# Moving the right-hand pools of a fused attention and two-MoE kernel by 160 and 224 bytes

## The chip, the cores and the metric

The kernel runs on one core of one Trainium2 chip. The metric is the device time of one execution in microseconds; several executions are timed and the median is given. One more execution is profiled, and the trace is of that one.

## The reference

Attention for 4 batches of 8 heads, 576 positions, 64 per head, with a threshold: scores more than tau below their row's largest are cut off before the softmax. Its output, 2304 tokens of 512, goes through two feed-forward layers of width 2048, all in float32.

```python
scores = scale * np.matmul(q, k.transpose(0, 1, 3, 2))
thresh = np.max(scores, axis=-1, keepdims=True) - tau
scores = np.where(scores >= thresh, scores, -1000000000.0)
attn = np.exp(scores - np.max(scores, axis=-1, keepdims=True))
attn = attn / (np.sum(attn, axis=-1, keepdims=True) + 1e-09)
x = np.matmul(attn, v)                       # to [2304, 512]
h = x @ moe_w_in;  x = (h * np.clip(h + 3.0, 0.0, 6.0) / 6.0) @ moe_w_out
h = x @ moe2_w_in; x = (h / (1.0 + np.exp(-1.702 * h))) @ moe2_w_out
```

## The kernel before

Every float32 matrix is split into a high and a low part that TensorE reads in its fast float32 form, and a product is made of three matmuls: high by high, high by low and low by high (`xh`, `xl`, `inhring`, `inlring` and so on). The stages overlap. Up to some 400 us, attention runs pair of heads by pair of heads: scores into PSUM tile `ps` (line 807, and 831 and 847 for the first batch), maximum, exponential and threshold into `e` (lines 863 to 867), transposes (`pk`, `et`, `tr`), the product with the values (lines 1009 and 1025). The first layer's first half of the weights is multiplied in between (lines 1087 and 1112, the helpers `gated` and `out_mm`). From 400 us to 650 us comes the first layer's second half (1087, 1112 and the wide form, 1202). From 650 us on comes the second layer in two passes, in a form with seven products in place of eight on quarter blocks (`hidden2`, line 1321, and the product with the second matrix, line 1457).

The order of the work is worked out while the program is built. A planner (`Plan`) holds every operation with its engine and its dependencies; a packed table of ranks (`RANKS`) and a table of exchanged engines (`SWAPS`) decide the order. Each engine gets its own queue, in which instructions run in the written order and wait on semaphores. All large transfers are issued from SyncE's queue.

On-chip memory is filled from two ends. Pools are opened on the left (`const`, then `LEFT` and `MIDDLE`, later `LAST`) and on the right (`RIGHT` during attention, then `LATE`, then `END` and `xv`). A pool that is closed gives its room to the next one on its side. A constant of 4 bytes takes 32, and a tile's size is otherwise a multiple of 64, nearly always of 256, so a whole side has one remainder. These are the addresses in bytes within a partition, as the program's build places them:

| pool | side | first and last byte's end | remainder of a tile's start modulo 256 |
|---|---|---|---|
| const: id, id2, two, tau, sc, nt, big, half, gate | left | 16,512 to 18,208 | 128 (id, two, tau), others differ |
| ring1: weights, first ring | left | 18,208 to 83,744 | 32 |
| gp, tp: g, t | left | 83,744 to 109,344 | 32 |
| xr, x1: attention's result, its parts | left | 109,344 to 132,384 | 32 |
| gl, ct (after xr and x1 are closed) | left | 109,344 to 134,944 | 32 |
| raw, st, e, et (attention) | right | 154,848 to 229,344 | 224 |
| bt, stg or tr (attention) | right | 138,208 to 154,848 | 224, and 32 past a multiple of 64 |
| ring2: weights, second ring (after attention) | right | 163,808 to 229,344 | 224 |
| yc, stg2, later xs with xab or xv | right | 135,136 to 163,808 | 224 |

The change touches the lists of pools, `change()`, which closes attention's pools and opens those of `LATE`, the line that makes the small constants (545), and the operation `TL` (line 1654). `TL` runs one activation of the kind that the second layer needs, on a single column, behind the last exponential of attention; its result, written to `gate_b`, is read by nobody.

Of the kernel before, what the change touches and what calls it, by code (L numbers as in the profile page):

```python
# [10 lines left out]
F32 = mybir.dt.float32  # L11
# [4 lines left out]
ACTF = mybir.ActivationFunctionType  # L16
# [3 lines left out]
P = 128  # L20


PE, ACT, DVE, POOL, SP, DMA = range(6)
# [377 lines left out]
def tile_top_attention_moe_moe2(  # L401
# [13 lines left out]
    nc = tc.nc  # L415
# [13 lines left out]
    LEFT = ("ring1", "gp", "tp")  # L429
    MIDDLE = ("xr", "x1")  # L430
    RIGHT = ("raw", "st", "e", "et", "bt", "stg")
    LATE = ("ring2", "yc", "stg2", "py")
    LAST = ("gl", "ct")
    END = ("xs", "xab")
    attention, middle, staging, staging2, blocks = (ExitStack() for _ in range(5))
    pools = {n: ctx.enter_context(tc.tile_pool(name=n, bufs=1)) for n in ("const",) + LEFT}
    pools.update((n, middle.enter_context(tc.tile_pool(name=n, bufs=1))) for n in MIDDLE)
    pools["pm"] = ctx.enter_context(tc.tile_pool(name="pm", bufs=1, space=PS))
    for n in RIGHT:
        pools[n] = (staging if n == "stg" else attention).enter_context(tc.tile_pool(name=n, bufs=1, side="right"))  # L440
# [6 lines left out]
    def change():  # L447
        attention.close()
        for n in LATE:
            pools[n] = (staging2 if n == "stg2" else ctx).enter_context(tc.tile_pool(name=n, bufs=1, space=PS) if n == "py" else tc.tile_pool(name=n, bufs=1, side="right"))  # L450

    def change2():
        middle.close()
        for n in LAST:
            pools[n] = ctx.enter_context(tc.tile_pool(name=n, bufs=1))
# [10 lines left out]
    pl = Plan()  # L466
    changed = []

    def add(eng, cost, time, name, fn, rd=(), wr=(), touch=(), alt=None):
        op = pl.add(eng, cost, time, fn, rd, wr, name, touch)  # L470
        op.alt = alt
        for c, names in changed:
            if any(b.pool in names for b in op.bufs):
                op.deps.add(c)
        return op

    def move(time, name, nbytes, fn, rd=(), wr=(), eng=SP):

        op = add(eng, 590, time, name, fn, rd, wr)
        add(DMA, nbytes / 360 * PACE.get(name, 1.0), time, name, lambda: None, rd, wr).deps.add(op)  # L480

    def buf(tag, ring, pool, shape, dt=F32):
        b = Buf(pl, tag, ring, None, pool)
        b.make = lambda: pools[pool].tile(shape, dt, tag=f"{tag}{b.idx % ring}" if ring > 1 else tag, name=tag, bufs=1)
        return b
# [22 lines left out]
    def const(name, shape):  # L508
        b = buf(name, 1, "const", shape)
        b.t  # L510
        return b
# [30 lines left out]


    id_b, id2_b, two_b = const("id", [P, P]), const("id2", [P, 64]), const("two", [P, P])
    tau_b, sc_b, nt_b, big_b, half_b, gate_b = (const(n, [P, 64 if n == "gate" else 1]) for n in ("tau", "sc", "nt", "big", "half", "gate"))
    move(-30000, "tau", 4 * P, lambda: nc.sync.dma_start(out=tau_b.t, in_=tau), [], [tau_b])
    move(-25000, "id", 4 * P * P, lambda: nc.sync.dma_start(out=id_b.t, in_=ident), [], [id_b])
    add(DVE, 69, -30000, "sc", lambda: nc.vector.tensor_scalar(out=sc_b.t, in0=tau_b.t, scalar1=0.0, scalar2=scale, op0=ALU.is_ge, op1=ALU.mult), [tau_b], [sc_b])
# [1008 lines left out]
    t, u = 0, 0  # L1557
    for b in range(B):
        halves_ = []
        for j in range(H // 2):  # L1560
            halves_.append(unit(u, b, j, t))
            if u < FULL:
                halves_[j](0)
                t, u = t + 2700 * 4, u + 1
            else:
                halves_[j]()
                t, u = t + 2700 * 9, u + 1
# [8 lines left out]
        else:  # L1576
            for p in range(2):
                moe_a(b, p, t + 6000)

    changed.append((add(SP, 0, 0, "change", change), LATE))  # L1580
    changed[-1][0].deps |= {o for o in pl.ops if any(x.pool in RIGHT + ("tr", "ps") for x in o.bufs)}
    chunks = [(B - 1, 0), (B - 1, 1)]
# [68 lines left out]
                fetch(w[i], kept[4 + i], t - 30000 + 9000 * i)  # L1651
                w[i] = products(w[i])

    add(ACT, 1500, t, "TL", lambda: nc.scalar.activation(out=gate_b.t[:, :1], in_=half_b.t, func=ACTF.Gelu_apprx_sigmoid), [half_b], [gate_b]).deps |= {o for o in pl.ops if o.name == "X"}

    def tie(ins, first):
        if ins is not None and first is not None:
# [68 lines left out]
```

## Time and profile before

| | |
|---|---|
| median of 3 runs | 1023.88 us |
| lowest and highest run | 1023.46 and 1024.68 us |
| the profiled execution | 1023.98 us |
| its span, first to last instruction | 1022.2 us |
| TensorE busy | 1009.4 us, 99% of the span |
| VectorE, ScalarE, GpSimd busy | 80%, 65%, 54% |

The span is shorter than the execution's own time by what lies before the first and after the last instruction. "Busy" counts from an instruction's start to its end; matmuls are pipelined, so their ends overlap and a busy TensorE can still be slower or faster per matmul. In the chain that ended last, a piece of one line with its count of matmuls gives the time from matmul to matmul.

### The profile page before, as it was taken

Reading aid. Unit: us, or ns where it says so; the run is one execution under the profiler, and the core shown is the slowest. Engines: PE = TensorE matmul, PEld = TensorE weight load, DVE = VectorE, ACT = ScalarE, POOL = GpSimd, SP = SyncE. Lnnn points to the kernel's source line nnn. Section 1 sums busy time; section 2 is a strip of 40 time slices with the busy share of each in tenths; the row PEclk is TensorE's granted clock in tenths of the full one; section 3 lists DMA queues with packets and bytes.
Section 4 is the critical chain, followed back from the end, with each engine's and each line's share of the span. In section 5 each row is a group of like instructions: output and inputs, shape, how many; then the busy total and the mean of one; then the engine's idle time right before and its main releaser. Section 6 shows DMA issues by size and latency. Waiting matters only on the chain.

```text
span 1022.2 us, 21304 instructions
## 1 busy us (share of the span) xinstructions
PE 1009.4 (99%) x7530; PEld 942.7 (92%) x7530; DVE 813.3 (80%) x1728; ACT 668.6 (65%) x1399; POOL 547.0 (54%) x661
## 2 busy tenths in 40 slices
PE   8999999999999999999999999999999999999998
PEld 6787888798979898999999999999999999999998
DVE  7999999999889994678888767757688988665654
ACT  5998887776776765655455443567667767555563
POOL 5677776665756543656434344355544345536432
PEclk9999999999999999999999999999999999999999
DMA  8434476685868665446766665837465896443412
GB/s 234 122 115 144 140 193 179 178 230 176 250 193 220 181 201 159 134 150 206 241 190 213 199 206 181 291 129 244 160 212 193 269 300 209 154 156 106 154 41 83
DMA packets 114059, 187.45 MB, mean 183 GB/s; under 512 B 10913, under 2 KB 64289, under 8 KB 111905
## 3 DMA queue, kind: packets, MB, share of 16 engines
q1 hardware_dynamic: 113808, 185.80, 59.1%
q8 instruction: 59, 0.97, 0.4%
q14 instruction: 48, 0.39, 0.1%
q10 hardware_dynamic: 144, 0.29, 0.1%
HBM read 117.77 MB, written 68.29 MB: 182 GB/s over the span
## 4 chain that ended last, share of the span: by engine, by line
PE 90%; DVE 4%; DMA 3%; ACT 2%; issue 1%; SPq 0%; POOL 0%; DVEq 0%; ACTq 0%
PE pm L1321 17%; PE pm L1087 11%; PE py L1457 10%; PE pm L1112 9%; PE py L1112 8%; PE pm L1202 7%; PE ps L807 6%; PE pm L1457 6%; PE pm L1025 5%; PE pm L933 4%; PE pm L1009 2%; PE ps L831 1%; PE ps L847 1%; PE pm L1029 1%; DMA kept<-inhring 1%
## 5 line engine op out<-in xcount | busy, mean ns | idle before, releaser
L863 DVE TENSOR_REDUCE nm<-ps 128x1 f32<-128x576 f32 x144 | 106.0, 749 | 12.2 <-PE ps L807 7.3
L535 POOL TENSOR_TENSOR g<-t,g 128x256 fp32r<-128x256 f32 (+2 forms) x84 | 73.0, 870 | 79.4 <-ACT g L532 43.5
L866 ACT ACTIVATE e<-ps,nm 128x576 f32<-128x576 f32 x128 | 93.0, 737 | 29.5 <-DVE nm L863 25.6
L1112 PE MATMUL pm<-g,outhring 128*128 128x256 f32 (+1 forms) x512 | 106.8, 300 | 0.0
L867 DVE SCALAR_TENSOR_TENSOR e<-ps,th,e 128x576 f32<-128x576 f32 x128 | 102.4, 809 | 4.9 <-ACT e L866 3.4
L532 ACT ACTIVATE g<-t 128x256 fp32r<-128x256 f32 (+3 forms) x173 | 83.5, 489 | 28.3 <-DVE t L1214 14.9
L1112 PE MATMUL py<-g,outhring 128*128 128x432 f32 (+2 forms) x384 | 97.2, 337 | 1.0 <-DVE yc L535 0.6
L1087 PE MATMUL pm<-xh,inhring 128*128 128x256 f32 (+1 forms) x320 | 97.1, 303 | 0.2
L1087 PE MATMUL pm<-xl,inhring 128*128 128x256 f32 (+1 forms) x320 | 94.4, 295 | 0.0
L1087 PE MATMUL pm<-xh,inlring 128*128 128x256 f32 (+1 forms) x320 | 94.4, 295 | 0.0
L535 POOL TENSOR_TENSOR wmstg<-wmstg,wrstg 128x512 uint32<-128x512 uint32 x40 | 55.4, 1388 | 66.1 <-DVE wmstg L589 28.8
L1112 PEld LDWEIGHTS pm<-g,outhring 128*128 128x128 f32 x512 | 82.0, 189 | 2.9 <-issue 2.5
L807 PE MATMUL ps<-kqv 128*128 128x288 f32 x480 | 81.4, 302 | 1.4 <-DVE e L867 0.5
L1112 PE MATMUL pm<-g,outlring 128*128 128x256 f32 (+1 forms) x256 | 75.8, 296 | 0.1
L807 PEld LDWEIGHTS ps<-kqv 128*128 128x128 f32 x480 | 68.1, 190 | 7.6 <-PE pm L1029 2.0
L1112 PEld LDWEIGHTS py<-g,outhring 128*128 128x128 f32 x384 | 68.2, 188 | 4.1 <-DVE yc L535 0.9
L535 POOL TENSOR_TENSOR kqv<-qk,kqv 128x576 fp32r<-128x576 f32 (+1 forms) x39 | 56.4, 1446 | 19.2 <-PE pm L1029 8.4
L1400 ACT ACTIVATE t<-c 128x512 f32<-128x512 f32 (+1 forms) x80 | 46.2, 582 | 31.0 <-DVE c L535 29.9
L1112 PE MATMUL py<-g,outlring 128*128 128x432 f32 (+2 forms) x192 | 64.6, 336 | 0.0
L1087 PEld LDWEIGHTS pm<-xh,inhring 128*128 128x128 f32 x320 | 60.5, 189 | 2.7 <-PE pm L1667 0.7
L1087 PEld LDWEIGHTS pm<-xl,inhring 128*128 128x128 f32 x320 | 60.5, 189 | 0.0
L1087 PEld LDWEIGHTS pm<-xh,inlring 128*128 128x128 f32 x320 | 60.4, 189 | 0.0
(316 smaller groups left out, 3571.9 us busy)
## 6 DMA issues: line engine op xcount, KB each, us to landing
turned<-tr SPq DMA_DIRECT2D x16, 1024.0 KB, 4.0
et<-turned SPq DMA_DIRECT2D x64, 256.0 KB, 6.2
wrawstg<-in_w1i_dram SPq DMA_DIRECT2D x16, 512.0 KB, 4.1
wrawstg<-in_w1o_dram SPq DMA_DIRECT2D x16, 512.0 KB, 3.8
wrawstg<-in_w2i_dram SPq DMA_DIRECT2D x16, 512.0 KB, 4.0
wrawstg<-in_w2o_dram SPq DMA_DIRECT2D x16, 512.0 KB, 4.1
qk<-in_k_dram SPq DMA_DIRECT2D x24, 288.0 KB, 3.4
qk<-in_q_dram SPq DMA_DIRECT2D x24, 288.0 KB, 3.8
```

What stands on the lines that cost most here:

```text
L532: return lambda: nc.scalar.activation(out=o(), in_=i(), func=ACTF.Copy, **kw)
L535: return lambda: (nc.vector if eng == DVE else nc.gpsimd).tensor_tensor(out=o(), in0=a(), in1=b(), op=op)
L807: nc.tensor.matmul(ps.t[:, i, :SH], q, w[hd].t[:, i * SH:(i + 1) * SH], start=a, stop=z)
L863: add(DVE, 672, K("R", s), "R", lambda: nc.vector.tensor_reduce(out=nm.t[:, c], in_=ps.t[:, :, :SH], op=ALU.max, axis=AX.XY, negate=True), ...
L866: add(ACT, 624, K("X", s), "X", lambda: nc.scalar.activation(out=ev(), in_=ps.t[:, :, :SH], func=ACTF.Exp, bias=nm.t[:, c]), [ps, (nm, s)] ...
L867: add(DVE, 736, K("M", s), "M", lambda: nc.vector.scalar_tensor_tensor(out=ev(), in0=ps.t[:, :, :SH], scalar=th.t[:, c], in1=ev(), op0=ALU ...
L1025: nc.tensor.matmul(pv[p].t[64 * hd:64 * hd + 64, :CH[p][1]], v_(k, hd), et_m(p, turned)[:, hd, k], start=k == 0, stop=False)
L1087: nc.tensor.matmul(ph.t[:, :n], a, v, start=(cc == 0 and i == 0), stop=(cc == KC - 1 and i == 2))
L1112: nc.tensor.matmul(py.t[:, :n], a, v, start=(st and i == 0), stop=(sp and i == 2))
L1202: nc.tensor.matmul(ph.t[:, :n], a, v, start=(cc == 0 and q == 0), stop=(cc == KC - 1 and q == 2))
L1321: nc.tensor.matmul(half(i)(), u.t[:, ws], v.t[:, xv], start=False, stop=True, skip_group_check=True)
L1457: nc.tensor.matmul(to, u.t[:, ws], v.t[:, at:at + n], start=(st and j == 0 and cc == 0 and o is not None), stop=(sp and j == 2), skip_grou ...
```

## The change

Two tiles of padding that nothing uses are put on the right side: `edge`, 40 floats (160 bytes), ahead of all right pools, for the whole program; and `gap`, 16 floats (64 bytes), between the second ring and the pools below it, from `change()` on. `TL`'s result goes to tau's tile, and the tile `gate`, 64 floats, is no longer made. The operations, their engines and their order stay.

```diff
-    LATE = ("ring2", "yc", "stg2", "py")
+    LATE = ("ring2", "gap", "yc", "stg2", "py")
...
+    pools["edge"] = ctx.enter_context(tc.tile_pool(name="edge", bufs=1, side="right"))
+    pools["edge"].tile([P, 40], F32, tag="edge", name="edge", bufs=1)
     pools["pm"] = ctx.enter_context(tc.tile_pool(name="pm", bufs=1, space=PS))
     for n in RIGHT:
...
         for n in LATE:
             pools[n] = (staging2 if n == "stg2" else ctx).enter_context(tc.tile_pool(name=n, bufs=1, space=PS) if n == "py" else tc.tile_pool(name=n, bufs=1, side="right"))
+        pools["gap"].tile([P, 16], F32, tag="gap", name="gap", bufs=1)
...
-    tau_b, sc_b, nt_b, big_b, half_b, gate_b = (const(n, [P, 64 if n == "gate" else 1]) for n in ("tau", "sc", "nt", "big", "half", "gate"))
+    tau_b, sc_b, nt_b, big_b, half_b = (const(n, [P, 1]) for n in ("tau", "sc", "nt", "big", "half"))
...
-    add(ACT, 1500, t, "TL", lambda: nc.scalar.activation(out=gate_b.t[:, :1], in_=half_b.t, func=ACTF.Gelu_apprx_sigmoid), [half_b], [gate_b]).deps |= {o for o in pl.ops if o.name == "X"}
+    add(ACT, 1500, t, "TL", lambda: nc.scalar.activation(out=tau_b.t, in_=half_b.t, func=ACTF.Gelu_apprx_sigmoid), [half_b], [tau_b]).deps |= {o for o in pl.ops if o.name == "X"}
```

## Rows read from the trace of the kernel before

**Rows 1.** The page's head: span, busy time by engine, TensorE's granted clock by slice.
```profile
span 1022.2 us, 21304 instructions
...
PE 1009.4 (99%) x7530; PEld 942.7 (92%) x7530; DVE 813.3 (80%) x1728; ACT 668.6 (65%) x1399; POOL 547.0 (54%) x661
...
PEclk9999999999999999999999999999999999999999
```

**Rows 2.** The page's chain that ended last, shares by engine.
```profile
PE 90%; DVE 4%; DMA 3%; ACT 2%; issue 1%; SPq 0%; POOL 0%; DVEq 0%; ACTq 0%
```

**Rows 3.** Waits of TensorE's matmuls: us in total, times, longest us.
```profile
PE pm L1667 <- DVE two L553: 1.4, 1, 1.4
PE pm L933 <- DVE et L937: 1.1, 1, 1.1
PE ps L831 <- DMA qk<-in_k_dram: 1.1, 1, 1.1
...
PE py L1457 <- DVE gl L535: 0.2, 1, 0.2
```

**Rows 4.** The tile gate: duration in ns, first and last start in us.
```profile
L1654 ACT ACTIVATE gate<-half x1: 204/204/204, 388.7 to 388.7; 128x1 f32<-128x1 f32 x1
```

**Rows 5.** The tile tau, its last reader.
```profile
L550 DVE TENSOR_SCALAR nt<-tau,big x1: 210/210/210, 4.7 to 4.7; 128x1 f32<-128x1 f32 x1
```

**Rows 6.** Transfers by line: count, KB each, median us to landing.
```profile
xkept<-yc SPq DMA_DIRECT2D x16, 256.0 KB, 2.3
xkept<-xhxs SPq DMA_DIRECT2D x14, 256.0 KB, 2.3
...
xr<-x1d SPq DMA_DIRECT2D x16, 216.0 KB, 2.9
...
yc<-ypd SPq DMA_DIRECT2D x12, 216.0 KB, 4.8
...
y2d<-outhring SPq DMA_DIRECT2D x5, 256.0 KB, 2.4
...
out_dram<-inlring SPq DMA_DIRECT2D x5, 256.0 KB, 2.2
...
xkept<-inhring SPq DMA_DIRECT2D x4, 256.0 KB, 2.1
xkept<-outhring SPq DMA_DIRECT2D x4, 256.0 KB, 2.4
...
out_dram<-inhring SPq DMA_DIRECT2D x4, 256.0 KB, 2.2
```

**Rows 7.** ScalarE's groups by shape: count, busy us, mean ns, idle before.
```profile
L532 ACT ACTIVATE g<-c 128x512 fp32r<-128x512 f32 x64 | 40.0, 628 | 14.1 <-POOL c L535 10.4 <-DVE c L535 2.8 <-PE pm L1321 0.8
...
L532 ACT ACTIVATE outhring<-outlring 128x512 fp32r<-128x512 f32 x13 | 8.1, 624 | 4.9 <-DMA outlring<-kept 4.9
...
L532 ACT ACTIVATE xhxs<-xa 128x512 fp32r<-128x512 f32 x9 | 5.7, 629 | 2.7 <-DVE xa L535 1.5 <-DMA xa<-x2d 1.2
```

**Rows 8.** Stretches of 25 us: busy by engine, clock, DMA share, GB/s.
```profile
825.00:850.00 25.00, 24.87 (x212) 24.67 (x211) 22.25 (x45) 17.37 (x41) 12.44 (x12) 1.00 0.93 309
...
975.00:1000.00 25.00, 25.00 (x213) 24.61 (x212) 11.15 (x22) 16.43 (x41) 10.52 (x11) 1.00 0.02 7
```

**Rows 9.** The late stretch: all instructions, then line 1321's alone.
```profile
650.00:1016.00 366.00, 365.14 (x3079) 362.39 (x3078) 262.42 (x487) 236.11 (x553) 171.21 (x171) 1.00 0.54 180
...
650.00:1016.00 366.00, 203.96 (x1536) 189.50 (x1535) 1.00 0.54 180
```

**Rows 10.** Pieces of the chain: start us, us, what, count.
```profile
209.97 2.15 PE pm L1087 x18
...
453.48 2.83 PE pm L1087 x24
...
746.44 2.04 PE py L1457 x18
...
926.98 2.12 PE py L1457 x18
```

## The prediction

> **What bounds the kernel now.** I read the page's head first: TensorE is busy for 1009.4 us of a span of 1022.2 us, at a granted clock of nine tenths or more in all slices, while VectorE is at 80%, ScalarE at 65% and GpSimd at 54% [rows 1]. The chain that ended last says the same: 90% of it is TensorE, 4% VectorE, 3% transfers, 2% ScalarE [rows 2]. So the reader is to see a kernel whose length is the length of one engine's queue. All that a change can win without making a matmul itself quicker lies in the 1022.2 - 1009.4 = 12.8 us in which TensorE is idle. The view of waits, kept to TensorE, shows how little of that is somebody's lateness: eleven entries, from 1.4 us down to 0.2 us, 7.4 us in all, one of them a transfer (1.1 us) [rows 3]. The rest is the start, the tail and gaps too short to count as a wait.
>
> The diff moves no instruction in any queue. It moves addresses. So three prices matter: of a transfer, of an instruction on VectorE, ScalarE or GpSimd, and of a matmul, each at another address.
>
> **The change part by part.**
>
> *Where things go.* The result of the activation in line 1654 goes into tau's tile, and the 256 bytes of the gate table vanish from the constants. The left pools thus go down by 256 bytes: they keep their remainder of 32 modulo 256. On the right, 160 bytes at the edge take the pools from remainder 224 to 64, and 64 more bytes below the weights' second ring take yc, the staging pools and the x pools that follow from 224 to 0. So every right tile now begins at a multiple of 64 where it began 32 past one, and left and right, 64 bytes apart modulo 256 (224 to 32), are afterwards 32 apart (32 to 64, or 0 to 32). The free space allows it: the lowest right pool begins at 135,136 and the highest left one ends at 134,944, and 192 + 256 - 224 = 224 bytes stay free.
>
> *The two tiles of padding.* Nothing writes or reads them: no instruction, no semaphore, 0 us. Bound: 0 on both sides.
>
> *The activation.* It is one instruction of 204 ns on ScalarE at 388.7 us, and no one waits for it [rows 4]. In its new place it must come behind tau's three readers, the last of which starts at 4.7 us [rows 5], 384 us earlier. Nothing stands behind a new wait. 0 us; if the cover were gone and it sat in TensorE's path whole, +0.2 us.
>
> *The transfers.* Their number, bytes and order stay; only the address on the chip's side moves. The trace has both remainders that are in use now, 32 (left) and 224 (right), for stores of the same 256 KB. To the left belong out_dram<-inhring and <-inlring at 2.2 us and y2d<-outhring at 2.4; to the right xkept<-inhring at 2.1, <-xhxs and <-yc at 2.3, <-outhring at 2.4 [rows 6]. The two sides overlap. The loads of 216 KB differ, 2.9 us to xr on the left and 4.8 to yc on the right [rows 6], but these go out in other stretches beside other transfers, and one row per side can't tell crowding from address. The trace has no 256 KB transfer at a multiple of 64. From the stores, I take 0 us. Bounds: if the 8% between the 2.2 of the left and the 2.4 of the right were the address's doing, 8% of the transfers' 3% of the chain (31 us) would be 2.5 us won; and the gain can't pass 12.8 us. A loss has the same reach by the same rows, 2.1 against 2.4 at one remainder.
>
> The Trainium skill speaks for a gain here. Its page "DMA: Bandwidth & Descriptors", section "How a descriptor splits into AXI transactions", says that a transaction starts at a 256-byte boundary, that a descriptor which starts elsewhere fetches the bytes below it for nothing, and that a beat is 32 bytes. By it a row of 2,048 bytes costs 71 beats at remainder 224, 65 at 32, 66 at 64 and 64 at 0: an estimate of 7 to 10% off every right transfer, 2 to 3 us off those in the chain. It would also have the right stores 9% longer than the left now, and the rows don't show that [rows 6]: 2.1 to 2.4 against 2.2 to 2.4. The sum goes by the rows.
>
> *VectorE, ScalarE and GpSimd.* ScalarE shares no instruction's time with another engine in this trace, so its rows are the cleanest: a copy of 128x512 takes 628 ns from left to left (g<-c), 629 from right to right (xhxs<-xa), 624 inside the weights' rings (outhring<-outlring) [rows 7]. A remainder of 32 and one of 224 cost the same within 5 ns, which is what the same row spreads over. I take 0. These engines also have 20 to 46% of slack behind a TensorE that is idle for 1%, so some nanoseconds on each would hardly show.
>
> *The matmuls.* Here the leverage is: 3,079 matmuls in the 366 us from 650 us on [rows 9], nearly all of 256 columns, so 1 ns on each is 3.1 us. The trace does show more than one price for the same shape. The pieces of the chain, divided by their counts: 2.15/18 = 119.4 ns at 210 us (weights in the left ring, moving x on the left), 2.83/24 = 117.9 ns at 453 us (same line, weights in the right ring), 2.04/18 = 113.3 ns at 746 us, 2.12/18 = 117.8 ns at 927 us [rows 10]. The last two are the same line 1457 with weights in the same right ring and moving g on the left, with the same remainders. So TensorE has two paces, some 4.5 ns apart, that the same addresses show both of: pace there isn't set by remainder. Nor do transfers set it: in a stretch with the DMA engines 93% busy TensorE got through 212 instructions in 25 us, in one with 2% through 213 [rows 8]. I take 0 us. Bounds: the mean of the late part is 365.14/3079 = 118.6 ns with its waits; all of it at 113.3 would win 16.3 us; all of it dearer by the 1.5 ns that lie between 119.4 and 117.9 would lose 4.6 us.
>
> *Sum.* Padding 0, activation 0, transfers 0, engines 0, matmuls 0. The profiled execution took 1023.98 us, its span 1022.2 and 1.78 around it; with nothing added it stays 1023.98, 0.1 above the median of the runs. I forecast the median again: **1023.9 us**.
>
> **The rivals.**
>
> 1. *No part of the chip that matters here reads the new remainder.* 1023.9 us. For it: the equal rows of stores, of ScalarE and of the two paces at one address. Against: no row of this trace has a large tile at a multiple of 64, so all the evidence is from 32 and 224. That the compiler drops the untouched padding, so that nothing moves, ends here too.
>
> 2. *Right transfers get shorter.* Place: the 31 us of the chain that are transfers. Price: 8%, 2.5 us: 1021.4 us. The page of the skill named above stands for this one. Against it is that TensorE itself waited for a transfer for 1.1 us only [rows 3], and that most such links in the chain run beside a busy TensorE.
>
> 3. *Matmuls whose moving operand or weights lie on the right take the fast pace more often.* Place: line 1321 streams from the right pools, 1,536 matmuls [rows 9]. If each went from 117.8 to 113.3 ns, 6.9 us would go: 1017.0 us. For it: the fast pace exists. Against: it exists at the old addresses, on operands of either side.
>
> 4. *Slower: left and right streams get into each other's way.* A matmul reads weights from one side while it streams from the other. The dearest row, 119.4 ns, has both on the left at one remainder; the same line with weights 64 bytes off costs 117.9 [rows 10]. If nearness costs, 32 bytes apart is nearer than 64, and the late part pays up to the same 1.5 ns on 3,079: +4.6 us, 1028.5 us. It decides from 2.05/3079 = 0.67 ns on. Against: the dear row is also early, where the other engines are busiest.
>
> **How the numbers follow.** About 0.2%, 2.05 us, is what a measurement of this kernel can tell from no change; the three runs of before lie within 0.12%. The chances: rival 1 at 0.57, 2 at 0.10, 3 at 0.17, 4 at 0.16. Rivals 2 and 3 are faster by over 0.2%, so 0.27, 0.57 and 0.16. The likeliest gives the time. The range must leave out no more than 0.2: it goes down to 1018.5, which takes in rival 2 and those of rival 3 where not all matmuls change pace, and up to 1028.5, the whole price of rival 4. The likeliest alone would be 1022 to 1026.
>
> **What would show it.** Right: the same count of instructions on each engine, 256 KB stores between 2.1 and 2.4 us from both sides, ScalarE copies of 128x512 at 624 to 629 ns, TensorE busy within 2 us of 1009.4, and pieces of the chain still at both 113 and 118 ns. Rival 2 would show as right loads and stores below 2.1 us and the transfers' share of the chain below 3%; rival 3 as pieces of line 1321 mostly at 113 ns; rival 4 as pieces of lines 1321 and 1457 at 119 or more. What makes the forecast wrong is a step that the trace of before can't see: any engine that pays for a start 32 past a multiple of 64 and no longer does, or a shift of a few tens of nanoseconds somewhere that changes which matmuls run at which pace.

## The result, and the profile after

The changed kernel takes 1031.3 us (median of 4 runs, 1031.18 to 1031.39) against 1023.83 us before: ratio 1.0076, interval 1.0064 to 1.0088. It is slower by 7.5 us, and the forecast of 1023.9 us, with a range up to 1028.5, was wrong.

The head of the page after, and the shares of the chain that ended last, answer to [rows 1, 2]:

```profile
span 1029.6 us, 21304 instructions
...
PE 1017.1 (99%) x7530; PEld 949.4 (92%) x7530; DVE 816.1 (79%) x1728; ACT 667.4 (65%) x1399; POOL 546.6 (53%) x661
...
PEclk9999999999999999999999999999999999999999
...
PE 87%; DVE 5%; ACT 3%; DMA 2%; POOL 2%; issue 1%; SPq 0%; DVEq 0%; ACTq 0%; POOLq 0%
```

The counts of instructions are those of before, the clock is still full, and the span has grown by 7.4 us. TensorE's busy time has grown by 7.7 us. So TensorE doesn't wait longer: the same 7,530 matmuls and loads of weights take longer. TensorE's waits after say so too (us in total, times, longest); there are 13 of them now with 7.5 us in all, where [rows 3] had 11 with 7.4:

```profile
PE pm L1670 <- DVE two L556: 1.4, 1, 1.4
PE pm L936 <- DVE et L940: 1.1, 1, 1.1
PE ps L834 <- DMA qk<-in_k_dram: 0.9, 1, 0.9
...
PE py L1460 <- DVE gl L538: 0.2, 1, 0.2
```

(The changed file's line numbers lie 3 higher. In the text I keep the numbers of before.)

The transfers after, by line, and ScalarE's groups by shape (count, busy us, mean ns), against [rows 6, 7]:

```profile
xkept<-yc SPq DMA_DIRECT2D x16, 256.0 KB, 2.2
xkept<-xhxs SPq DMA_DIRECT2D x14, 256.0 KB, 2.3
...
xr<-x1d SPq DMA_DIRECT2D x16, 216.0 KB, 3.3
...
yc<-ypd SPq DMA_DIRECT2D x12, 216.0 KB, 5.0
...
y2d<-outhring SPq DMA_DIRECT2D x5, 256.0 KB, 2.8
...
out_dram<-inlring SPq DMA_DIRECT2D x5, 256.0 KB, 2.2
```

```profile
L535 ACT ACTIVATE g<-c 128x512 fp32r<-128x512 f32 x64 | 39.9, 627 | 13.8 <-POOL c L538 10.0 <-DVE c L538 2.6 <-PE pm L1324 0.8
...
L535 ACT ACTIVATE xhxs<-xa 128x512 fp32r<-128x512 f32 x9 | 5.6, 628 | 2.2 <-DVE xa L538 1.5 <-DMA xa<-x2d 0.6
```

The right stores keep their 2.2 to 2.3 us, the copies their 627 and 628 ns.

Where TensorE lost the time is in the pieces of the chain. These are of the kernel before, then of the one after (start us, us, what, count):

```profile
503.32 9.40 PE pm L1202 x48
...
578.92 7.05 PE pm L1202 x36
...
748.48 2.04 PE pm L1457 x18
```

```profile
209.06 2.14 PE pm L1090 x18
...
453.14 2.84 PE pm L1090 x24
...
502.94 9.59 PE pm L1205 x48
...
579.77 7.20 PE pm L1205 x36
...
750.05 2.13 PE py L1460 x18
752.18 2.13 PE pm L1460 x18
...
933.06 2.13 PE py L1460 x18
```

The reader is to see three stages. Early, at 209 us, nothing has changed (2.14 to [rows 10]'s 2.15). In the wide form of 432 columns (lines 1202 and 1112) a matmul went from 9.40/48 = 195.8 to 9.59/48 = 199.8 ns. In the late part the pair of pieces that took 2.04 us each, [rows 10]'s at 746.44 and the one behind it, takes 2.13: from 113.3 to 118.3 ns. The late stretch as a whole, against [rows 9]:

```profile
650.00:1024.00 374.00, 373.12 (x3096) 370.55 (x3095) 266.25 (x488) 236.81 (x555) 171.89 (x172) 1.00 0.53 177
```

That is 373.12/3096 = 120.5 ns per matmul, 118.6 before. The same matmul starts 0.4 us earlier than before at 503 us, 2.3 us later at 658 us and 7.35 us later at the end. So 2.7 us were lost in the wide stage and 5.1 in the late one.

### The profile page after: what moved, and what is told of

The parts are those of the page before. It is cut to its first block, busy times and chain, and to the rows that moved or that the text cites. A ratio compares the mean times of both kernels' runs of the same rounds, so it can differ in the third digit from the quotient of the medians.

```text
span 1029.6 us, 21304 instructions
## 1 busy us (share of the span) xinstructions
PE 1017.1 (99%) x7530; PEld 949.4 (92%) x7530; DVE 816.1 (79%) x1728; ACT 667.4 (65%) x1399; POOL 546.6 (53%) x661
## 4 chain that ended last, share of the span: by engine, by line
PE 87%; DVE 5%; ACT 3%; DMA 2%; POOL 2%; issue 1%; SPq 0%; DVEq 0%; ACTq 0%; POOLq 0%
PE pm L1324 18%; PE py L1460 11%; PE pm L1090 10%; PE py L1115 9%; PE pm L1115 8%; PE pm L1205 7%; PE pm L1460 6%; PE ps L810 5%; PE pm L1028 4%; PE pm L936 3%; PE pm L1012 1%; PE ps L834 1%; DVE nm L866 1%; DVE e L870 1%; PE pm L1032 1%
```

## The experiments

**How the intervals are read.** The busy time of a line leaves out where its matmuls overlap with others. So I took from the trace the time from each matmul's start to the next one's, by line and shape; an interval counts where both matmuls are of one line and at one distance (as defined next), and intervals over columns/2.4 + 25 ns, taken to hold a wait, are left out. **Distance** is the start of the weights less the start of the stream within a partition, modulo 256. It follows from the remainders in the table of pools and the bytes that a kernel adds, and only multiples of 32 were tried. Before, line 1457 and the wide form have weights at 224 and streams at 32: 192. Line 1321 has 32 less 224: 64. After, these are 32 and 32 (some 270 matmuls of line 1321 whose stream lies in the right ring: 224). Where weights and stream both lie on the left (lines 1087 and 1112 early), it is 0.

Each diff below is against the changed kernel; where the gap tile goes, its pool's name goes from `LATE` too.

**First four: which property of the addresses?** Theory A: the price follows the distance modulo 64. B: a right tile that starts at a multiple of 64 is dear. C: no price of addresses, only shifted waits.

32 bytes more among the left constants:

```diff
+    const("pad", [P, 8])
```

> The change, with one constant of 32 bytes more on the left, so that the left pools begin at remainder 64 modulo 256 (they stood at 32); right pools as in the change (64 and 0). All tiles then begin at a multiple of 64, and left and right at the same remainder modulo 64. Theory A (the price of a matmul follows from the distance between its weights and its stream: dear where they lie 32 apart modulo 64, cheap where they are equal): at least as fast as before, 1023.9 us or less; 769 or more TensorE instructions between 500 and 650 us. Theory B (a right tile that begins at a multiple of 64 is dear by itself): still 1031 us, 757 instructions.

The edge tile at 64 bytes, no gap tile:

```diff
-    pools["edge"].tile([P, 40], F32, tag="edge", name="edge", bufs=1)
+    pools["edge"].tile([P, 16], F32, tag="edge", name="edge", bufs=1)
...
-        pools["gap"].tile([P, 16], F32, tag="gap", name="gap", bufs=1)
```

> No gap, and an edge of 64 bytes in place of 160: all right pools at remainder 160, the left at 32, so 128 apart modulo 256 and equal modulo 64. A: 1023.9 us, as before. B: 1023.9 us, as no tile begins at a multiple of 64. If the distance counts modulo 128 or 256 (before it was 192), another time than 1023.9, and the lines 1202, 1321 and 1457 move together.

The change without its gap tile:

```diff
-        pools["gap"].tile([P, 16], F32, tag="gap", name="gap", bufs=1)
```

> The edge of 160 bytes without the gap: all right pools at remainder 64, the left at 32. A and B: as slow as the change, 1031 us, since right and left stay 32 apart modulo 64 and the right tiles begin at a multiple of 64. If the gap is what costs (only the pools below the second ring): line 1202 and line 1457, whose weights lie in the second ring, stay slow, and line 1321, which streams from below it, goes back to 204.1 us: 1029 us.

No edge tile, a gap tile of 32 bytes:

```diff
-    pools["edge"].tile([P, 40], F32, tag="edge", name="edge", bufs=1)
...
-        pools["gap"].tile([P, 16], F32, tag="gap", name="gap", bufs=1)
+        pools["gap"].tile([P, 8], F32, tag="gap", name="gap", bufs=1)
```

> No edge, and a gap of 32 bytes: attention's pools and the second ring at 224 as before, the pools below the ring at 192, so that only line 1321's streams change their distance to the left ring. A and B: line 1321 alone dearer, by the 1.5 us or somewhat more that the change cost it, lines 1202 and 1457 as before (81.1 and 198.2 us): 1025.5 to 1027 us. If the whole effect is a shift of waits (theory C), no line alone moves and the time stays within 2 us of 1023.9 with all lines a little changed.

Measured, with the kernel before on the same chip at 1022.52 us: 1027.68 (ratio 1.0052, interval 1.0037 to 1.0068), 1028.47 (1.0061, 1.0046 to 1.0077), 1027.02 (1.0049, 1.0032 to 1.0066) and 1024.4 us (1.0018, 1.0008 to 1.0028). A and B fall with the second kernel: equal modulo 64 and at no multiple of 64, and yet 6 us slower. C falls with the intervals, which moved line by line. The third kernel lost 4.5 us, where A and B gave it the change's whole loss of 7.5; the fourth's 1.9 us fits both. In the first kernel only the left side has moved against the change. The sums of TensorE's busy time by line (lines 1202, 1321, 1457) are, after and then in that kernel:

```profile
0.00:1035.00 1035.00, 82.81 (x384) 1.00 0.58 181
...
0.00:1035.00 1035.00, 205.64 (x1536) 1.00 0.58 181
...
0.00:1035.00 1035.00, 201.61 (x1536) 1.00 0.58 181
```

```profile
0.00:1035.00 1035.00, 81.32 (x384) 1.00 0.58 181
...
0.00:1035.00 1035.00, 203.37 (x1536) 1.00 0.58 181
...
0.00:1035.00 1035.00, 202.87 (x1536) 1.00 0.58 181
```

32 bytes on the left made line 1457 dearer and lines 1202 and 1321 cheaper at once. Lines 1457 and 1202 had gone from distance 32 to 0, line 1321 from 32 to 64. Line 1457 now shows 119.1 ns, the price that the early matmuls, also at 0, always had (119.5). The other three fit in: line 1321 showed 118.5 ns at 128, 117.0 at 224 and 117.8 at 96, line 1457 118.4 at 128, 118.3 at 32 and still 116.1 at 192. That is theory D: the distance modulo 256 sets the pace, whichever side the weights lie on.

**Second four: distance or place?** Theory E: a remainder of one side decides by itself.

Both sides moved, so that no pool stands where it stood and the distances are those of before:

```diff
-    pools["edge"].tile([P, 40], F32, tag="edge", name="edge", bufs=1)
+    pools["edge"].tile([P, 56], F32, tag="edge", name="edge", bufs=1)
...
-        pools["gap"].tile([P, 16], F32, tag="gap", name="gap", bufs=1)
...
+    const("pad", [P, 8])
```

> The change with 32 bytes more among the left constants and the right side moved down by 32 bytes as well: the left remainder is 64, the right ones 0 and 0, so no pool stands where it stood before, but the distances modulo 256 between weights and stream are those of the kernel before (192 for weights on the right, 64 for weights on the left). Theory D (the pace of a matmul follows the distance from its stream's start to its weights' start modulo 256, and nothing else of the addresses): within 1 us of the kernel before, 256-column intervals of 116 ns in both late lines and 196 ns for 432 columns. Theory E (the remainder of the right pools, or of the left ones, decides by itself; in the runs so far a right remainder of 0 or 64 and a left one of 64 each went with a dear line): 3 to 8 us slower, L1457's line at 118 to 119 ns.

Distance 64 on both sides:

```diff
-    pools["edge"].tile([P, 40], F32, tag="edge", name="edge", bufs=1)
+    pools["edge"].tile([P, 32], F32, tag="edge", name="edge", bufs=1)
...
-        pools["gap"].tile([P, 16], F32, tag="gap", name="gap", bufs=1)
+        pools["gap"].tile([P, 32], F32, tag="gap", name="gap", bufs=1)
```

> Edge tile 128 bytes, gap tile 128 bytes: right remainder 96, lower pools 224, distances weights less stream 64 on both sides. Theory D, if distances 64 and 192 are alike for both lines: 256-column intervals of 116 ns in both late lines; the 432-column ones were not seen at 64 and lie between 194 and 200 ns (763 of them), so 1.3 us faster to 3.2 us slower than before. Theory E, and D with 192 alone good for weights on the right: L1457's line at 118 to 119 ns, 3 to 4 us slower or more.

The early matmuls taken off distance 0:

```diff
-    LEFT = ("ring1", "gp", "tp")
+    LEFT = ("ring1", "front", "gp", "tp")
...
+    pools["front"].tile([P, 48], F32, tag="front", name="front", bufs=1)
...
-    pools["edge"].tile([P, 40], F32, tag="edge", name="edge", bufs=1)
+    pools["edge"].tile([P, 16], F32, tag="edge", name="edge", bufs=1)
```

> A pool of 192 bytes is put between the left weights' ring and the streams on the left, edge tile 64, gap tile 64: the early matmuls, whose weights and stream both lie on the left at distance 0 and take 119.5 ns in every run so far, are now at distance 64; the late lines have 192 on either side, and some 270 matmuls of the left-weights line whose stream lies in the right ring fall to 128. Theory D: some 647 early 256-column matmuls gain 3.3 ns each (2.1 us), the 270 lose 2.3 ns each (0.6 us): 1.5 us faster than before, early intervals at 116 to 117 ns. Rival (the early pace comes of both operands lying on one side, whatever their distance): early intervals stay at 119.5 ns and the time is 0 to 1 us above before.

The change without its padding, so that tau's part stands alone:

```diff
-    pools["edge"].tile([P, 40], F32, tag="edge", name="edge", bufs=1)
...
-        pools["gap"].tile([P, 16], F32, tag="gap", name="gap", bufs=1)
```

> The change without its two tiles of padding: only the gate table's result goes to tau's constant, and what that frees among the constants stays as the change leaves it. Left remainder 32, right 224, lower pools 224, as in the kernel before. Theory D: the time before within 1 us, all intervals as before. Rival (the activation into tau's constant costs some of the loss): up to 1 us above before with unchanged intervals.

Measured, with before at 1022.33 us: 1022.11 (ratio 1.0001, interval 0.9992 to 1.0010), 1022.91 (1.0003, 0.9993 to 1.0012), 1025.88 (1.0033, 1.0022 to 1.0045) and 1022.59 us (1.0006, 0.9997 to 1.0016). The first is the decisive one: a left remainder of 64 and right ones of 0, each of which had gone with a dear line, and with the distances of before the whole loss is gone (115.9, 116.3 and 195.9 ns). The sums by line (1202, 1321, 1457) are those of the kernel before, here ahead of this kernel's:

```profile
0.00:1035.00 1035.00, 81.12 (x384) 1.00 0.59 181
...
0.00:1035.00 1035.00, 204.11 (x1536) 1.00 0.59 181
...
0.00:1035.00 1035.00, 198.15 (x1536) 1.00 0.59 181
```

```profile
0.00:1035.00 1035.00, 81.27 (x384) 1.00 0.57 181
...
0.00:1035.00 1035.00, 203.58 (x1536) 1.00 0.57 181
...
0.00:1035.00 1035.00, 198.03 (x1536) 1.00 0.57 181
```

E falls: what counts is where weights and stream lie to each other. The second met its time, but not by its parts: line 1457 showed 117.1 ns where D said 116, and 193.4 ns for 432 columns made up for it. The last clears the activation.

The third shows where D was too simple: 1.5 us faster than before was expected, and it was 3.5 us slower. Early the intervals fell as expected, from 119.5 to 115.3 ns. But with 192 on both sides the late lines rose to 117.9 and 117.7. The same distance, 192, had given 116.2 in line 1457 before. The intervals of a row of matmuls show why. This is the timeline of TensorE in the kernel before and in the one after, in the same row (start us, us, instruction):

```profile
746.62 0.28 PE L1457 MATMUL py<-g,inhring 128*128 128x256 f32 x1
746.73 0.28 PE L1457 MATMUL py<-gl,inhring 128*128 128x256 f32 x1
746.85 0.28 PE L1457 MATMUL py<-g,inlring 128*128 128x256 f32 x1
746.96 0.28 PE L1457 MATMUL py<-g,outhring 128*128 128x256 f32 x1
```

```profile
750.25 0.28 PE L1460 MATMUL py<-g,inhring 128*128 128x256 f32 x1
750.37 0.28 PE L1460 MATMUL py<-gl,inhring 128*128 128x256 f32 x1
750.49 0.28 PE L1460 MATMUL py<-g,inlring 128*128 128x256 f32 x1
750.61 0.28 PE L1460 MATMUL py<-g,outhring 128*128 128x256 f32 x1
```

A start every 0.113 us there, every 0.12 here. At 64 and at 192 a row can run at 113 to 114 ns or at 118. Over all fourteen kernels, 367 of the 1,012 rows at these two distances (a row: consecutive matmuls of one line at one distance, here with eight or more intervals read) have a mean of 115 ns or less; of the 973 at the other six distances none has, and the lowest is 116.2. At 192 a row keeps the pace that it began with (360 of 368 rows of 12 and more matmuls, by their first and last six intervals); at 64 three in four do (471 of 635). The share of line 1457's intervals of 115 ns or less is 41% before, 3% after and 0% in the third kernel. Two kernels with the same distances also find the quick pace in different rows. The row that takes 2.04 us in [rows 10] takes 2.12 in the kernel with both sides moved, and an earlier one, 2.12 before, takes 2.04:

```profile
688.91 2.12 PE pm L1457 x18
```

```profile
687.37 2.04 PE pm L1460 x18
...
744.94 2.12 PE py L1460 x18
```

The traces show more of this than the means do: a row's pace depends on the row ahead of it. Call a row quick at its end if its last three intervals have a mean of 115.5 ns or less, and take all late rows of six and more matmuls. In the kernel before, line 1457 (at 192) goes on at the pace of the row of line 1321 ahead: behind a quick one 56 of 56 rows end quick, behind a slow one 57 of 64 slow. Line 1321 (at 64) turns it over: behind a quick row of line 1457, 53 of 63 end slow, behind a slow one 45 of 56 end quick. That gives both paces about half of the rows. With 192 on both sides (the third kernel) hardly a row turns quick: 2 of 184 behind a slow one.

**Last four: a version that is faster, and the distances not yet seen.** If D holds, the early distance of 64 can be had with the late distances of before (192 and 64). Against the kernel that took the early matmuls off 0, only the gap tile differs:

```diff
-        pools["gap"].tile([P, 16], F32, tag="gap", name="gap", bufs=1)
+        pools["gap"].tile([P, 48], F32, tag="gap", name="gap", bufs=1)
```

> The pool of 192 bytes between the left ring and the left streams again, edge tile 64, gap tile 192: early weights less stream 64, late right weights less left stream 192, late left weights less the streams of the lower right pools 64, as in the kernel before; only some 270 matmuls that stream out of the right ring stand at 128. Theory D with two paces: at 64 and at 192 a row of matmuls can run at 113 to 114 ns or at 118, and the late lines find the quick one in about half their rows when 64 and 192 take turns. So early intervals of 115 ns (693 of them, 4.2 ns less each, 2.9 us), the late lines back near 116.2, the 270 dearer by 2.3 ns (0.6 us): 2.3 us faster than before, some 1,020 us. Rival (moving the left streams costs the late lines by itself, as in the run with 192 on both sides): late lines at 117.7 to 118, 3 us slower than before.

The same with the right weights at 64 as well (`front` 48, gap tile as in the change):

```diff
-    pools["edge"].tile([P, 40], F32, tag="edge", name="edge", bufs=1)
+    pools["edge"].tile([P, 48], F32, tag="edge", name="edge", bufs=1)
```

> As the run with the early distance at 64, but edge tile 192, gap tile 64: early 64, late right weights 64, late left weights 64, and the 270 at 0. Theory D: early 115 ns as there (2.9 us), 432 columns at 193.4 ns as in the run with 64 on both sides (763 by 2.3 ns, 1.8 us), L1457's line at 117.1 (1,412 by 0.9, 1.3 us lost), the 270 at 119 (0.7 us lost): 2.7 us faster than before. Rival as for the other: late lines at 118, 0 to 1 us slower.

Distance 160 on both sides:

```diff
-    pools["edge"].tile([P, 40], F32, tag="edge", name="edge", bufs=1)
+    pools["edge"].tile([P, 8], F32, tag="edge", name="edge", bufs=1)
```

> Edge tile 32, gap tile 64: weights less stream 160 for right weights, and 160 for left weights. Theory D: 160 is none of the two good distances (64, 192), so both late lines at 117 to 119 ns without rows at 113; 1,412 by 1 to 3 ns and 1,320 by 1 to 3 ns, 3 to 8 us slower, with 432 columns (not seen at 160) between 193 and 200 ns, so 1 to 11 us slower in all. Rival (the loss comes of distances under 64 or of 128 alone): within 1 us of before.

224 and 0:

```diff
-    pools["edge"].tile([P, 40], F32, tag="edge", name="edge", bufs=1)
+    pools["edge"].tile([P, 56], F32, tag="edge", name="edge", bufs=1)
...
-        pools["gap"].tile([P, 16], F32, tag="gap", name="gap", bufs=1)
+        pools["gap"].tile([P, 56], F32, tag="gap", name="gap", bufs=1)
```

> Edge tile 224, gap tile 224: weights less stream 224 for right weights, 0 for left weights. Theory D: L1321's line at 119 to 119.5 ns as the early matmuls at 0 (some 1,050 of them, 3 ns each, 3 us; the rest, out of the right ring, at 32: 0.5 us), L1457's line at 117.0 as the left weights showed at 224 (1,412 by 0.9 ns, 1.3 us), 432 columns not seen at 224, between 193 and 200 ns (1.7 us less to 3.2 us more): 3 to 8 us slower. Rival (a distance of 0 is dear only where both operands lie on one side): L1321's line near 116.3, 0 to 4 us slower.

Measured, with before at 1022.34 us: 1018.65 (ratio 0.9963, interval 0.9949 to 0.9977), 1019.44 (0.9969, 0.9958 to 0.9981), 1033.25 (1.0108, 1.0093 to 1.0122) and 1027.45 us (1.0052, 1.0038 to 1.0067). Each lies on D's side of its rival. At 224 and 0 line 1321 showed 119.0 ns and line 1457 117.0, as expected from other lines at these distances. Two of them were off in their parts: with 64 everywhere lines 1087 and 1112 showed 116.8 ns (115 expected) and line 1457 114.9 (117.1 expected), misses of opposite sign behind a time that was met; at 160 the late lines showed 119.3 and 119.6, over the 117 to 119 expected, and the time lies at the top of its range. The first beats both kernels, the one before by 3.7 us and the changed one, by the two ratios, by some 11. An early piece with both operands on the left, and the late pair, in its chain:

```profile
116.02 2.73 PE pm L1116 x24
...
745.13 2.04 PE py L1461 x18
747.17 2.04 PE pm L1461 x18
```

against the early one in the kernel before:

```profile
116.44 2.87 PE pm L1112 x24
```

2.73/24 = 113.8 against 119.6 ns, and nothing but an address lies between them. It gained more than expected, because the late lines came down to 114.9 and 114.7 ns (expected near 116.2).

A second distance goes with that: from the last stream of a row to the first weights of the other line's row behind it. In the kernel before it is 0 at both changes of line; here it is 192 into line 1457 and 64 into line 1321, with the distances inside the rows as before. Of the rows of line 1321 at 64 behind a quick one, 43 of 54 now end quick, where 10 of 63 did. The two kernels with 64 inside the late rows differ in the same way: in the one with 64 everywhere it is 64 at these changes too, and 105 of 122 rows behind a quick one end quick; in the one of the second four it is 128 and 0, and 2 of 70 do. Their line 1457 takes 114.9 and 117.1 ns at one and the same distance. No run changes this second distance alone, so that it is the cause is argued and not shown.

All kernels together, mean interval in ns by distance (lowest and highest mean of a kernel's line, with at least 180 intervals in each):

```
distance     256 columns                        432 columns
  0          118.1 to 119.6                     195.9
 32          118.2 to 118.4                     199.7 and 199.9
 64          114.7 to 117.1  (two paces)        193.4
 96          117.8 and 118.3                    not seen
128          118.4 to 118.9                     194.0
160          119.3 to 119.6                     198.9
192          114.9 to 117.9  (two paces)        195.7 to 195.9
224          117.0 to 117.2                     196.7
```

Lines of 320 columns don't care: 146.4 to 147.0 ns at all seven distances that they had.

## Why the prediction was wrong, step by step

*What bounds the kernel*: right. TensorE's busy time grew by 7.7 us and the span by 7.4.

*Padding and activation at 0*: right. The activation into tau's tile took 203 ns at 388.2 us, and the kernel that has it alone is within its interval of before:

```profile
L1657 ACT ACTIVATE tau<-half x1: 203/203/203, 388.2 to 388.2; 128x1 f32<-128x1 f32 x1
```

*Transfers, VectorE, ScalarE, GpSimd at 0*: nothing speaks against it. The rows above are those of before within 0.1 us for the right stores and 1 ns for the copies, and TensorE's busy time grew by as much as the span. The left store y2d<-outhring, whose remainder the change leaves alone, went from 2.4 to 2.8 us, so these medians move by 0.4 us where no address on the chip's side moved. By the Trainium skill's page "DMA: Bandwidth & Descriptors", section "How a descriptor splits into AXI transactions", a row of xkept<-yc, which now starts on a multiple of 256 bytes, takes 64 beats in place of 71; if all of its time went by beats, it would have gone from 2.3 to an estimated 2.3 x 64/71 = 2.1 us. The trace says 2.2, and 2.3 for xkept<-xhxs, which had 2.3 before: by rows that move by 0.4 the rule is neither seen nor refuted, and TensorE's waits for transfers (1.1 us before, 0.9 after) had nothing to give. The 0 was right on thinner ground than the prediction says: its rows are the quicker stores of either side, and the same view has others of 256 KB at up to 4.8 us on the right and 3.9 on the left, a spread far over the 8% that they were to rule out.

```profile
y2d<-inlring SPq DMA_DIRECT2D x5, 256.0 KB, 3.9
...
xkept<-inlring SPq DMA_DIRECT2D x4, 256.0 KB, 4.8
```

*The matmuls at 0*: **this step failed**. It went "two paces that the same addresses show both of: pace there isn't set by remainder". The first half is true. The conclusion doesn't follow: addresses can decide whether the quick pace is to be had at all. At 192 and 64, where the kernel before stood, both paces exist; at 32, where the change put both late lines, only the slow one is left (no piece of either in the chain after is under 118.3 ns). The two rows that I compared had the same distance, so they could say nothing on what another distance does. The pair of rows that did differ in distance, 119.4 and 117.9 ns on line 1087, was laid to the stage and to rival 4.

*Rival 4* had the right mechanism, a price on the distance between weights and stream, and the right sign. Its size was short: 1.5 ns on 3,079 late matmuls, 4.6 us. The late lines paid 2.1 ns (line 1457, 116.2 to 118.3) and 2.0 (line 1321 at 32, 116.3 to 118.3; its 270 at 224 paid 0.9), 5.1 us in all by the starts. The wide stage before 650 us, which the rival left out, paid some 4.2 ns on 768 matmuls: 2.9 us on the 690 whose interval could be read, 2.7 by the starts. Its law, that nearness costs, is wrong: 160 is as dear as 0, 128 is dear too, and 64 is the best. Its mark in the profile, "pieces at 119 or more", wasn't met; the mark would have been that no piece of line 1457 stays at 113.

*Rival 3* asked for the fast pace more often. It came less often under this change, and more often in the first two of the last four kernels: the same lever, the other way.

What stays open is where in TensorE the nanoseconds go. Since weights are loaded beside the streams (949.4 us of loads and 1017.1 of matmuls in one span of 1029.6), two reads of one memory that meet would fit. The Trainium skill's page "TensorE: Matmul & The Clock Gate", section "Step-by-step: what each phase is for", says the contrary: "Loading the next tile's weights doesn't steal SBUF read bandwidth from the running matmul." The runs here differ in addresses alone and pay up to 5 ns for it at 256 columns, so the pair of operands isn't free of each other; whether it is the reads that meet was not tried. Nor is it settled why, in the kernel before, line 1321 turns over the pace of the row ahead and line 1457 keeps it.

## What to carry to other kernels

Where TensorE is busy for 99%, the start addresses of weights and stream are part of the tuning: here they move the time by -0.4 to +1.1% with every instruction the same, and one number, their distance modulo 256, tells most of what a padding will do. It doesn't tell all: with 192, a distance that has the quick pace, in both late lines, the kernel was 3.5 us slower than before, and the same 64 gave line 1457 114.9 and 117.1 ns. When two paces are seen at one address, ask what would take the quick one away before concluding that the address is of no account. And read the time from start to start by line and shape: the busy share says 99% before, after and in the fastest kernel alike.

## What the runs showed that I had not expected

How far a period of 256 bytes goes: at line 1457 before, intervals are the same when the distance is split further, modulo 1,024 (116.19 and 116.19 ns, by the weights that follow on a stream). In the first of the first four kernels, where that line stands at 0, its two halves differ, 118.6 and 119.5, and so do those of line 1321 before, 115.8 and 116.9, though there they also stand at different places of a row. So the distance modulo 256 carries most of the pace, and whether all of it isn't shown. 320 columns are indifferent within 0.6 ns, while 432 columns range over 6.5 ns, with 32 as the dearest and 64 as the cheapest. And kernels with the same distances inside and between their rows differ in which rows are quick. Each kernel left one trace, so whether executions of one program differ in this as well isn't shown.
